# Attention and experts on one core: each half expert serves all four batches in one pass, with the input parts streamed from DRAM

## The chip, the core and the metric

The kernel runs on one core of a Trainium2 chip. The metric is the device time of one execution in microseconds (us). Three executions of the kernel before gave 2418.21, 2427.02 and 2414.76 us, median 2418.21 us. One more execution was taken with the profiler; its time was 2428.88 us and its span, from the first instruction to the last, 2427.1 us.

Five engines work side by side, each through its own list of instructions in order: PE (TensorE, the matmuls), DVE (VectorE), ACT (ScalarE), POOL (GpSimd) and SP (SyncE, which here issues all the transfers). PEld is the loading of a matmul's stationary operand.

## What is computed

```python
# attention: B, H, S, D = 4, 8, 768, 64 with 16 clusters
mask = q_assign[:, :, :, None] == k_assign[:, :, None, :]
attn = softmax(where(mask, q @ k.T / sqrt(D), -1e9))
x = (attn @ v) as [B * S, H * D] = [3072, 512]
# mixture of experts: E, DM, DF = 8, 512, 1024
P = exp(x @ w_gate - max)
for _ in range(8):
    P /= P.sum(1, keepdims=True) + 1e-9
    P /= P.sum(0, keepdims=True) + 1e-9
    P *= N / E
out = sum over e of P[:, e:e+1] * (relu(x @ w1[e]) @ w2[e])
```

The gates P are normalised eight times by rows (over the experts) and by columns (over all 3072 tokens of all four batches), so that no gate is known before the attention of the last batch has ended.

## The kernel before, in words

**Attention** comes first, head after head, and leaves each batch's output transposed in `xT`; `out_batch` (line 934) stores it to DRAM (`xd`), takes the logits of its gates, and for batch 0 alone its largest magnitude (`amx`, line 940), from which `first_x` makes the operands of batch 0 while attention still runs. In the same time `scan_first` (line 975) reads the weights of experts 0 and 1 once, for their largest magnitude.

**The experts** are split in two ways. Each matrix product is done by Strassen's scheme in the form with seven products: a 2 by 2 block product takes seven block matmuls ("pieces", m = 0 to 6 or n = 0 to 6) in place of eight, and pays with sums and differences of blocks. And each number is held as two float16 numbers, a high part (made on ACT) and a low part (what is left, made by a subtraction on DVE or POOL), so that a product takes three matmuls: high by high, high by low, low by high. So there are three preparations. Of a **weight** (`make_first`, line 1154, for w1; `make_second`, line 1197, for w2): load the raw block of 512 KB, scale it (ACT), four sums of blocks, and high and low parts of seven blocks in three steps (256, 512 and 1024 columns). Of the **input** of a batch (`next_x`, line 1282): four quarters `xq` are read from `xd`, four differences are taken, and seven parts `xs` (named B11, T1, T2, B22, T3, B21, T4) are split in high and low. Of the **hidden layer**: see below.

The work is a list of 64 **units** (line 1036): a unit is one batch b, one expert e and one half g of its 1024 hidden columns. A half expert is two weight tiles `wa` and two `wb` (f2 = 2g and 2g + 1). In each unit `layer1` (line 1334) runs seven pieces for each of two halves j, six matmuls of 384 columns each, 84 in all; `layer2` (line 1516) runs seven pieces in two parts, 18 matmuls of 256 columns a piece, 126 in all. Between them stand, for each j, on ACT the evictions `c` (line 1370) and the high parts of `h` (lines 1379 and 1388); on DVE the sums with the evicted products (`plus`, line 1373, three of them, one input in PSUM), three low parts of relu(c) (`split_raw`, line 1381, both inputs in SBUF) and four sums (`sums_of`, line 1464, both inputs in SBUF); on POOL or DVE four more low parts (`split_sum`, line 1390). `collect` (line 1546) adds each finished product, weighted by its gate, into the output on DVE (lines 1571 to 1577), 21 instructions a unit.

The 64 units are in two passes: batches 0 and 1 through all eight experts (32 units), then batches 2 and 3. Weights are made in the first pass, four tiles of each kind an expert, and stored to DRAM (`wd1`, `wd2`, 64 stores of 896 KB); the second pass loads them back (`load_first`, `load_second`, 64 loads). The input parts of two batches stay in SBUF for a whole pass. `scan` (line 1258) reads the raw weights of experts 2 to 7 again for their largest magnitude: eight loads of 512 KB and eight reductions on DVE (line 286) an expert.

**The gates** (line 1076): a maximum over all logits, an exponential, and eight rounds of seven DVE lines, two of which multiply the whole table `pr` (lines 1104 and 1119), with one small matmul (line 1111) for the column sums in the middle of each round.

**The order of the instructions** is set by a planner (lines 60 to 150) when the program is written. Each preparation is a process that asks for an engine with a cost in microseconds; the planner lets the engine that comes free first take the process with the smallest key (its due time), and the engines then keep that order. `LEAD` is the time, in the planner's clock, at which PE begins with the experts; `either(pool, dve)` offers a step to POOL and DVE, with a reluctance in microseconds added to DVE's. PE's own list is fixed: piece after piece of layer 1, and from piece 18 on one piece of layer 1 and one part of layer 2 by turns (`run_pe`, `LAG = 4`). The planner's costs are only what it plans with.

## Time and profile before

| | us |
|---|---|
| profiled execution | 2428.88 |
| its span | 2427.1 |
| median of three plain executions | 2418.21 |
| first matmul of the experts begins | 560.85 |
| last matmul of the experts begins | 2422.14 |
| PE busy in the span | 2295.4 (95%) |
| DVE busy | 2055.1 (85%) |
| POOL busy | 1278.9 (53%) |
| ACT busy | 1155.4 (48%) |

The profile's page gives busy times and the span in forty slices; other views of the same trace group instructions by line and shape in a stretch of time, list who waited for whom, follow the chain of waits that ended last, or give a table by stretches of time: busy time of each engine (with the number of its instructions in brackets), granted clock of PE as a share of full speed, busy share of the DMA engines, and GB/s. Times of instructions in a group may overlap by a few hundredths of a microsecond where one begins while the last one drains, so that a sum of them is somewhat more than the busy time.

### The profile page before, as it was taken

The numbers are of one execution on the slowest core, as the hardware profiler recorded it, in microseconds if no ns is written. First come the engines' busy times: TensorE is split into PE (matmuls) and PEld (weight loads), VectorE is DVE, ScalarE is ACT, GpSimd is POOL, SyncE is SP. The second block draws the span as 40 slices with busy tenths as digits, with TensorE's granted clock in tenths as the row PEclk, the third lists the DMA queues.
The fourth block names the chain that finished last, engine by engine and source line by source line (L and its number), as shares of the span: only waits on it lengthen the run. The fifth ranks groups of instructions, "written<-read, shape, count | busy, mean of one in ns | idle before, by whom it ended". The sixth has DMA issues, their size and how long they took to land.

```text
span 2427.1 us, 42887 instructions
## 1 busy us (share of the span) xinstructions
PE 2295.4 (95%) x16244; PEld 1618.8 (67%) x16244; DVE 2055.1 (85%) x3806; ACT 1155.4 (48%) x2300; POOL 1278.9 (53%) x1261
## 2 busy tenths in 40 slices
PE   6999999995899999999999999999999999999998
PEld 3655555552576677767776767777777777777776
DVE  7878777877999999999999999987777777777776
ACT  3554555554466555555555555443333333333332
POOL 4676766667678767666766666422232222222221
PEclk7999999997899999999999999999999999999999
DMA  8555454523234435343434223312111122112101
GB/s 186 132 128 142 94 121 90 136 71 137 98 116 152 145 121 171 119 153 122 144 122 139 96 94 124 118 61 92 62 62 62 62 79 90 61 67 72 62 31 53
DMA packets 145408, 254.02 MB, mean 105 GB/s; under 512 B 59592, under 2 KB 99632, under 8 KB 144688
## 3 DMA queue, kind: packets, MB, share of 16 engines
q1 hardware_dynamic: 145200, 251.28, 33.5%
q8 instruction: 127, 2.08, 0.4%
q14 instruction: 81, 0.66, 0.1%
HBM read 151.04 MB, written 71.30 MB: 92 GB/s over the span
## 4 chain that ended last, share of the span: by engine, by line
PE 69%; DVE 24%; issue 3%; ACT 1%; DMA 1%; SPq 1%; POOL 1%; DVEq 0%; ACTq 0%; POOLq 0%
PE a_ps L1350 15%; PE a_ps L1533 11%; PE ac_ps L1533 9%; PE c_ps L1533 8%; PE c_ps L1350 7%; DVE acc L1577 5%; PE av_ps L827 4%; PE b_ps L1350 4%; DVE c L1464 3%; PE max_ps L700 3%; DVE h L1381 3%; PE exp_ps L768 2%; PE exp_ps L769 2%; DVE mrt L704 2%; DVE c L1373 1%
## 5 line engine op out<-in xcount | busy, mean ns | idle before, releaser
L1533 PEld LDWEIGHTS <-h 128*128 128x128 f16 x8064 | 791.4, 98 | 225.9 <-issue 40.8
L1350 PEld LDWEIGHTS <-wa 128*128 128x128 f16 x5376 | 528.5, 98 | 288.3 <-issue 37.3
L1390 POOL TENSOR_TENSOR h<-s,h 128x384 f16<-128x384 f32 x128 | 130.3, 1018 | 712.0 <-ACT h L1388 697.8
L1379 ACT ACTIVATE h<-c 128x384 f16<-128x384 f32 x384 | 200.7, 523 | 536.0 <-DVE c L1373 535.6
L1350 PE MATMUL a_ps<-xsT,wa 128*128 128x384 f16 x2304 | 439.5, 327 | 13.8 <-ACT c L1370 7.0
L1533 PE MATMUL a_ps<-wb,h 128*128 128x256 f16 x3072 | 378.4, 273 | 12.8 <-DVE acc L1577 11.8
L1533 PE MATMUL ac_ps<-wb,h 128*128 128x256 f16 x2688 | 366.6, 273 | 3.2 <-DVE acc L1577 3.2
L1533 PE MATMUL c_ps<-wb,h 128*128 128x256 f16 x2304 | 288.1, 275 | 15.1 <-DVE acc L1577 12.3
L1577 DVE SCALAR_TENSOR_TENSOR acc<-a_ps,gates,acc 128x256 f32<-128x256 f32 x472 | 216.3, 476 | 81.9 <-PE a_ps L1533 80.8
L1381 DVE SCALAR_TENSOR_TENSOR h<-c,h 128x384 f16<-128x384 f32 x384 | 250.7, 655 | 8.6 <-ACT h L1379 8.6
L794 POOL TENSOR_TENSOR psum<-psum,pe 128x512 f32<-128x512 f32 (+1 forms) x208 | 221.2, 1082 | 53.1 <-ACT pe L775 38.4
L775 ACT ACTIVATE pe<-exp_ps 128x512 f32<-128x512 f32 x288 | 166.1, 597 | 126.3 <-PE exp_ps L769 109.0
L1390 POOL TENSOR_TENSOR h<-c,h 128x384 f16<-128x384 f32 x190 | 207.9, 1105 | 30.8 <-ACT h L1388 26.4
L1577 DVE SCALAR_TENSOR_TENSOR acc<-ac_ps,gates,acc 128x256 f32<-128x256 f32 x412 | 196.0, 476 | 30.9 <-PE ac_ps L1533 27.1
L704 DVE TENSOR_REDUCE mrt<-max_ps 128x1 f32<-128x512 f32 (+1 forms) x288 | 189.1, 682 | 27.3 <-PE max_ps L700 25.4
L1577 DVE SCALAR_TENSOR_TENSOR acc<-c_ps,gates,acc 128x256 f32<-128x256 f32 x352 | 155.4, 475 | 39.8 <-PE c_ps L1533 39.7
L1388 ACT CAST h<-c 128x384 f16<-128x384 f32 x256 | 130.1, 509 | 94.6 <-DVE c L1464 93.4
L1370 ACT ACTIVATE c<-a_ps 128x384 f32<-128x384 f32 x256 | 124.8, 487 | 88.3 <-PE a_ps L1350 86.5
L1350 PE MATMUL c_ps<-xsB,wa 128*128 128x384 f16 x768 | 148.5, 330 | 11.7 <-ACT c L1370 11.7
L1350 PE MATMUL b_ps<-xsB,wa 128*128 128x384 f16 x768 | 147.8, 329 | 0.0
L1350 PE MATMUL a_ps<-xsB,wa 128*128 128x384 f16 x768 | 146.7, 328 | 0.0
L1350 PE MATMUL c_ps<-xsT,wa 128*128 128x384 f16 x768 | 146.7, 328 | 0.0
(240 smaller groups left out, 3656.7 us busy)
## 6 DMA issues: line engine op xcount, KB each, us to landing
raw<-in_moe_w SPq DMA_DIRECT2D x112, 512.0 KB
wda<-wa SPq DMA_DIRECT2D x32, 896.0 KB
wdb<-wb SPq DMA_DIRECT2D x32, 896.0 KB
wa<-wda SPq DMA_DIRECT2D x32, 896.0 KB
wb<-wdb SPq DMA_DIRECT2D x32, 896.0 KB
scan<-in_moe_w SPq DMA_DIRECT2D x32, 256.0 KB
qn<-in_q SPq DMA_DIRECT2D x16, 384.0 KB
kn<-in_k SPq DMA_DIRECT2D x16, 384.0 KB
```

Source lines behind the costliest of these rows:

```text
L704: nc.vector.tensor_reduce(out=t["mr"][:, i0 : i0 + ni, ni - 1], in_=ps.rearrange("p (x c) -> p x c", x=ni), axis=AX, op=ALU.max)
L775: nc.scalar.activation(pe, ps.rearrange("p (x c) -> p x c", x=ni), AF.Exp, scale=SCALE)
L794: (nc.gpsimd if e == POOL else nc.vector).tensor_tensor(out=st[:, a:z], in0=old[a], in1=part, op=ALU.add)
L827: nc.tensor.matmul(av[o, a:z], vn[:, i, :], heads[t]["pe", c][:, i - i0], start=(i == 0), stop=False, skip_group_check=True)
L1350: nc.tensor.matmul(ps[:, 0:HB], wt[:, w_, a, c, :], xt[:, x_, c, :], start=(n in (0, 1, 5) and s_ == 0), stop=(s_ == len(steps) - 1), skip ...
L1370: nc.scalar.activation(t, ps[:, 0:HB], func, scale=KAPPA)
L1379: nc.scalar.activation(t[:, 0], c, AF.Relu)
L1381: nc.vector.scalar_tensor_tensor(out=t[:, 1], in0=c, scalar=0.0, in1=t[:, 0], op0=ALU.max, op1=ALU.subtract)
L1388: nc.scalar.copy(t[:, 0], c)
L1390: by(w).tensor_tensor(out=t[:, 1], in0=c, in1=t[:, 0], op=ALU.subtract)
L1533: nc.tensor.matmul(view(m, i), t[:, a_, i * P : (i + 1) * P], w[:, b_, x, :], start=(opens and n == 0 and i in (0, 2)), stop=(n == 5), ski ...
L1577: nc.vector.scalar_tensor_tensor(out=to, in0=src, scalar=gate[b, e][:, ti : ti + 1], in1=to, op0=ALU.mult, op1=ALU.add)
```

## The change

1. **One pass.** Units are ordered by expert: expert 0 batch after batch, both halves each; then for each expert and half the four batches, by turns downwards (3, 2, 1, 0) and upwards. A half expert's weights are made once, serve four units in a row and are dropped. The 64 stores and 64 loads of made weights are gone.
2. **Input parts streamed.** The seven parts of every batch are stored once in DRAM (`xsd`, 28 stores of 384 KB) and read back, seven loads of 384 KB, for each unit whose batch differs from the last one's (45 of the units: 315 loads). There are eleven places in SBUF for seven parts: each load takes the place of a part whose last use is over. Batches 1, 2 and 3 are split in the first units, one after the other, in the spaces of an output tile that isn't used yet; their split scales the quarters first (ACT) and takes low parts by a plain subtraction on POOL or DVE.
3. **Gates later and wider.** The gates begin 40 us later in the planner's clock, leave 2 us (`ROOM`) around each of their steps on PE, and do their two products of the whole table on POOL.
4. **The start.** `LEAD` is 32 in place of 25, and the planner takes the other engines as partly busy before it. The largest magnitude is taken of batches 0, 1 and 2 during attention (`LARGEST`), of batch 3 later. Expert 1 is scanned among the experts, no longer during attention.
5. **POOL or DVE.** From unit 8 on the reluctance towards DVE is 1.5 in place of 0.3. Raw blocks have three places in place of four, and the outputs of all four batches stay in SBUF.

The core of the diff:

```diff
-LEAD = 25.0
+LARGEST = 2
+LEAD, LOGITS, ROOM = 32.0, 40.0, 2.0
...
-            if b == 0:
+            if b <= LARGEST:
                 yield DVE, 3.3
+                amx = sm.tile([P, 1], F32, name="amx")
                 largest(amx, xts[b].rearrange("p c s -> p (c s)"))
...
-        for e in range(2):
-            plan.spawn(scan_first(e), urgency("values", nheads - 12 + 4 * e))
+        plan.spawn(scan_first(0), urgency("values", nheads - 12))
...
+    NRAW, NH = 3, 20
...
-    for c in range(B // 2):
-        for e in range(E):
-            turns = [(j, g) for g in range(NG2) for j in range(2)] if e else [(j, g) for j in range(2) for g in range(NG2)]
-            units += [(2 * c + j, e, g) for j, g in turns]
+    units = [(b, 0, g) for b in range(B) for g in range(NG2)]
+    for e in range(1, E):
+        for g in range(NG2):
+            turn = range(B - 1, -1, -1) if g % 2 == 0 else range(B)
+            units += [(b, e, g) for b in turn]
     NU = len(units)
+    FULL = NG2 * B
...
     def gates():
+        yield LOGITS
...
-            yield DVE, 0.4
-            nc.vector.tensor_tensor(out=pr, in0=pr, in1=r.unsqueeze(2).broadcast_to([P, NTT, E]), op=ALU.mult)
+            yield POOL, 0.6
+            nc.gpsimd.tensor_tensor(out=pr, in0=pr, in1=r.unsqueeze(2).broadcast_to([P, NTT, E]), op=ALU.mult)
...
             yield t_g
+            yield ROOM
             yield PE, 0.15
             ps = g_tile()
             nc.tensor.matmul(ps[:, 0:E], ones, c, start=True, stop=True)
+            yield ROOM
...
-    def either(pool, dve, reluctance=0.3):
-        return (POOL, pool), (DVE, dve, reluctance)
+    def either(pool, dve):
+        return (POOL, pool), (DVE, dve, 0.3 if ev["slot", FULL].time is None else 1.5)
...
-        yield SP, 0.6
-        nc.sync.dma_start(out=wd1[idx], in_=t.rearrange("p x a c f -> p (x a c f)"))
...
+    spots = [(3, r, q) for r in (1, 2) for q in (1, 2)]
+    t_spot = Tokens(len(spots))
...
     def next_x(b):
...
+        for o in XQ:
+            yield ev["xq", b, o]
+            yield ACT, 0.93
+            nc.scalar.activation(xq[o], xq[o], AF.Copy, scale=sx[:, b : b + 1])
+        for i, o in enumerate(XS):
             for t in LESS.get(o, ()):
                 w = yield either(2.25, 0.87)
                 less(*t, by(w))
+            yield t_spot
             yield ACT, 0.93
+            t = xs[b][o] = accp.tile([P, 2, KC, HB], F16, name=f"xt{b}{o}", tag=f"acc3{r}{q}")
+            nc.scalar.copy(t[:, 0], xq[o])
+            w = yield either(1.9, 0.9)
+            by(w).tensor_tensor(out=t[:, 1], in0=xq[o], in1=t[:, 0], op=ALU.subtract)
+            yield SP, 0.6
+            nc.sync.dma_start(out=xsd[b, o], in_=t.rearrange("p x c s -> p (x c s)"))
...
+    def load_x(u):
+        b = units[u][0]
+        if u > first_of[b] + 1:
+            yield from after(u - 2)
+        for n, o in enumerate(XS):
+            yield ev["xsd", b, o]
+            urgent(piece_time(u, n) - 9)
+            yield t_x
+            yield SP, 0.6
+            tag = free_x.pop(0)
+            t = xt[u, o] = pers.tile([P, 2, KC, HB], F16, name=f"x{u}{o}", tag=tag)
+            nc.sync.dma_start(out=t.rearrange("p x c s -> p (x c s)"), in_=xsd[b, o])
...
+        if j == 1 and u + 1 < NU and units[u + 1][0] != b:
+            free_x.append(xtag[u, x])
+            t_x.put(plan)
```

The planner makes the new order. At the start of the experts, DVE's list right behind the last sum of unit 0 (the row `c<-b_ps`), before (`pr`, `rsum` and `csum` are the gates' tables, `xs` and `xq` the parts of batch 1):

```order
L1373 SCALAR_TENSOR_TENSOR c_6476<-b_ps,c_6476 128x384
L1104 TENSOR_TENSOR pr<-pr,rsum 128x192
L307 SCALAR_TENSOR_TENSOR xsT_6537<-xqB_6270,sx,xsT_6537 128x768
L1107 TENSOR_REDUCE csum<-pr 128x8
L1464 SCALAR_TENSOR_TENSOR c_6371<-c_6371,s_6490 128x384
L1381 SCALAR_TENSOR_TENSOR h<-c_6504,h 128x384
L1381 SCALAR_TENSOR_TENSOR h<-c_6488,h 128x384
L1114 TENSOR_SCALAR csum_6594<-g_ps 128x8
L1115 RECIPROCAL csum_6594<-csum_6594 128x8
L1116 TENSOR_SCALAR csum_6594<-csum_6594 128x8
L1464 SCALAR_TENSOR_TENSOR s_6600<-c_6476,h_6560 128x384
```

The same place of DVE's list after the change (lines have moved: 1373 is 1429, 1381 is 1437, 1464 is 1520; 1262 is the low part of a `wb`, 1337 that of an input part):

```order
L1429 SCALAR_TENSOR_TENSOR c_6356<-b_ps,c_6356 128x384
L1437 SCALAR_TENSOR_TENSOR h<-c_6394,h 128x384
L1262 TENSOR_TENSOR wb<-raw,wb 128x256
L1124 TENSOR_SCALAR gneg<-g_ps 128x1
L1337 TENSOR_TENSOR xt1T_6396<-xqB_6191,xt1T_6396 128x768
L1520 SCALAR_TENSOR_TENSOR s_6466<-c_6356,h_6451 128x384
L1437 SCALAR_TENSOR_TENSOR h<-c_6371,h 128x384
L1520 SCALAR_TENSOR_TENSOR h_6451<-c_6371,h_6451 128x384
L1520 SCALAR_TENSOR_TENSOR c_6371<-c_6371,s_6466 128x384
L1520 SCALAR_TENSOR_TENSOR c_6394<-c_6394,c_6371 128x384
L1262 TENSOR_TENSOR wb<-sums,wb 128x1024
```

Before, the gates' third round stood between the hidden layer's steps here; now the gates are only at their maximum, and parts of weights stand there. From the logits to the last sum of unit 1 (the fourth row `c<-b_ps`) DVE had 146 instructions and has 82; from there to the last sum of unit 4 it had 150 and has 199.

The second place is POOL's list in the middle of the experts, before (`wa` and `sums` are weights, `h` the hidden layer's low parts):

```order
L1390 TENSOR_TENSOR h<-c_9748,h 128x384
L1181 TENSOR_TENSOR sums<-raw,sums 128x256
L1181 TENSOR_TENSOR sums<-raw 128x256
L1181 TENSOR_TENSOR sums<-sums,raw 128x256
L1189 TENSOR_TENSOR wa<-raw,wa 128x256
L1181 TENSOR_TENSOR sums<-raw 128x256
L1181 TENSOR_TENSOR sums<-raw,sums 128x256
L1189 TENSOR_TENSOR wa<-raw,wa 128x512
```

And after the change, in the middle of a later expert:

```order
L1446 TENSOR_TENSOR h<-h_19712,h 128x384
L1262 TENSOR_TENSOR wb<-sums,wb 128x1024
L1446 TENSOR_TENSOR h<-c_19597,h 128x384
L1446 TENSOR_TENSOR h<-c_19624,h 128x384
L1446 TENSOR_TENSOR h<-s_19895,h 128x384
L1446 TENSOR_TENSOR h<-h_19884,h 128x384
L1446 TENSOR_TENSOR h<-c_19776,h 128x384
L1446 TENSOR_TENSOR h<-c_19802,h 128x384
```

A unit has eight of these low parts of `h`. In the whole program POOL took 434 of the 512 before and takes 505 now; DVE took 78 and takes 7. The weights' sums and low parts were on DVE in 62 places and are in 16.

270 lines of the change are left out of this document (143 added, 127 removed).

## The prediction

> **What bounds the kernel now.** I read the slices of the page first, then the table by stretches, then who waited, then the groups of instructions by shape. In the page's forty slices (attention is the first nine or so) PE is full nearly everywhere, and DVE is full from slice 11 to slice 25 and less so afterwards:
>
> ```profile
> PE   6999999995899999999999999999999999999998
> DVE  7878777877999999999999999987777777777776
> ```
>
> The table by stretches says how much PE got done in each (start and end in us, length, then busy time and instructions of PE, PEld, DVE, ACT and POOL, PE's granted clock, busy share of the DMA engines, GB/s):
>
> ```profile
> 560.00:645.00 85.00, 50.50 (x266) 30.17 (x267) 77.28 (x147) 41.33 (x70) 66.12 (x55) 0.74 0.34 119
> 645.00:700.00 55.00, 55.00 (x425) 41.27 (x423) 48.87 (x96) 32.34 (x66) 32.47 (x34) 1.00 0.32 110
> 700.00:1500.00 800.00, 765.51 (x5758) 564.92 (x5756) 760.77 (x1340) 437.21 (x828) 552.59 (x493) 0.99 0.38 130
> 1500.00:1600.00 100.00, 97.32 (x738) 72.04 (x737) 95.42 (x177) 49.42 (x93) 46.36 (x37) 1.00 0.33 113
> 1600.00:2300.00 700.00, 700.00 (x5368) 524.98 (x5366) 545.68 (x1087) 267.41 (x561) 186.20 (x178) 1.00 0.20 71
> ```
>
> A unit has 84 + 126 = 210 matmuls. From 1600 to 2300 us, in the second pass, 5368 / 210 = 25.56 units took 700 us: 27.39 us a unit, with PE never idle. That is the floor, and the change leaves PE's work as it is. From 700 to 1500 us 5758 / 210 = 27.42 units took 800 us, 29.18 each; at the floor they'd have taken 751, so 49 us were lost there, and 3.7 more from 1500 to 1600 (738 matmuls are 96.3 us of work). From 645 to 700 nothing was lost (425 matmuls are 55.4 us). The stretch 560 to 645 holds the experts' start, with more of layer 1 than of layer 2, so I count by line (matmuls of that line, and by the chain what six of the one and six of the other take):
>
> ```profile
> 560.00:645.00 85.00, 37.10 (x162) 0.74 0.34 119
> 560.00:645.00 85.00, 12.76 (x82) 0.74 0.34 119
> ```
>
> ```profile
> 645.45 0.98 PE a_ps L1350 x6
> 646.43 0.66 PE ac_ps L1533 x6
> ```
>
> 162 x 0.163 + 82 x 0.110 = 35.4 us of work in 84 us (the first matmul is at 560.85): 49 us lost. All in all PE loses about 102 us among the experts, half at the start and half in the first pass. What it waits for at the start, by the timeline, and in the first pass, by the list of waits (total, times, longest):
>
> ```profile
> 607.39 2.08 PE L1350 MATMUL c_ps<-xsB,wa 128*128 128x384 f16 x6 [10.77 <-ACT c L1370]
> ...
> 635.21 0.60 PE L1111 MATMUL g_ps<-csum,ones 128*128 128x8 f32 x2 [7.28 <-DVE csum L1107]
> ```
>
> ```profile
> PEld L1533 <- issue: 36.7, 37, 2.9
> ```
>
> At the start PE stands before the gates' small matmuls and behind evictions that stand behind DVE; the six matmuls after such a wait take 2.08 us, about twice the usual, and the granted clock of the stretch is 0.74. In the first pass it stands before the loads of `h`, which DVE and POOL make. DVE is the engine behind both: 77.28 of 85 us, and 760.77 / 27.42 = 27.75 us a unit in the first pass against 545.68 / 25.56 = 21.35 in the second.
>
> **Part 1: the middle of the experts (units 5 to 60).** In the first pass a unit carries two sets of weights, later one. Three things change DVE's 21.35 us. The largest magnitudes of the weights come back, and low parts of `h` leave it:
>
> ```profile
> L286 DVE TENSOR_REDUCE am<-raw 128x1 f32<-128x1024 f32 x42 | 50.6, 1204 | 0.0
> L1464 DVE SCALAR_TENSOR_TENSOR c<-c,s 128x384 f32<-128x384 f32 x54 | 54.4, 1007 | 0.3
> L1464 DVE SCALAR_TENSOR_TENSOR s<-c,h 128x384 f32<-128x384 f32 x55 | 51.1, 929 | 0.6 <-ACT h L1370 0.6
> L1464 DVE SCALAR_TENSOR_TENSOR h<-c,h 128x384 f32<-128x384 f32 x55 | 42.3, 769 | 0.3
> L1381 DVE SCALAR_TENSOR_TENSOR h<-c,h 128x384 f16<-128x384 f32 x164 | 121.4, 745 | 2.5 <-ACT h L1379 2.4
> ```
>
> The same groups in the second pass (1700 to 2300 us, 22 units):
>
> ```profile
> L1381 DVE SCALAR_TENSOR_TENSOR h<-c,h 128x384 f16<-128x384 f32 x131 | 72.0, 550 | 4.3 <-ACT h L1379 4.3
> L1464 DVE SCALAR_TENSOR_TENSOR c<-c,s 128x384 f32<-128x384 f32 x44 | 32.7, 743 | 0.6
> L1464 DVE SCALAR_TENSOR_TENSOR h<-c,h 128x384 f32<-128x384 f32 x44 | 24.3, 553 | 1.3
> L1464 DVE SCALAR_TENSOR_TENSOR s<-c,h 128x384 f32<-128x384 f32 x44 | 24.1, 548 | 0.0
> L1390 DVE TENSOR_TENSOR h<-c,h 128x384 f16<-128x384 f32 x22 | 21.9, 994 | 1.1 <-ACT h L1388 1.1
> ```
>
> The scans are 56 over 56 units: +1.2 us. One low part of `h` a unit moves to POOL: -1.0. The third is a lengthening: these instructions read two tiles of SBUF, and they last longer where POOL is busier: six times 0.195, twice 0.264, 0.381 and 0.216, together 2.9 us a unit, between POOL's 186 / 700 = 27% and its 553 / 800 = 69%. POOL's load after the change, from its own rows:
>
> ```profile
> L1390 POOL TENSOR_TENSOR h<-c,h 128x384 f16<-128x384 f32 x73 | 78.9, 1090 | 14.3 <-ACT h L1388 14.2
> L1232 POOL TENSOR_TENSOR wb<-sums,wb 128x1024 f16<-128x1024 f32 x28 | 65.3, 2333 | 3.8 <-ACT wb L1230 3.4
> L1224 POOL TENSOR_TENSOR sums<-raw 128x256 f32<-128x256 f32 x47 | 40.6, 866 | 94.3 <-PE a_ps L1533 58.9 <-ACT raw L1213 35.5
> L1232 POOL TENSOR_TENSOR wb<-raw,wb 128x512 f16<-128x512 f32 x26 | 34.4, 1323 | 3.0 <-ACT wb L1230 3.0
> ```
>
> Eight low parts of `h` at 1.09 and one set of weights (four sums and a low part of 256 columns at 0.87, one at 1.32, one at 2.33) make 8.7 + 8.0 = 16.7 us of 27.4, 61%. In proportion the lengthening is 2.9 x (61 - 27) / (69 - 27) = 2.3 us. DVE then has 21.35 + 1.2 - 1.0 + 2.3 = 23.9 us a unit, 87%; the fullest units have three scans, 26.3, still below 27.4. What does PE lose at that? Nothing at 21.35, 1.8 us a unit at 27.75. A straight line gives 0.7 us, 40 us over 56 units; a threshold gives none. I take 13: DVE no longer falls behind for good, but the heavy units follow one another. So the 53 us lost from 700 to 1600 become 13 (0 to 40), though they are now spread over all units, the once undisturbed second half too.
>
> The Trainium skill, "SBUF — State Buffer", "Who interferes with whom", speaks against this part: a DVE instruction with two SBUF inputs and a GpSimd instruction that reads SBUF exclude one another, for a whole instruction at a time. The trace agrees on who suffers (the rows above); how much follows below as a rival.
>
> The transfers lie beside all this. The 64 stores and 64 loads of 896 KB (115 MB) go, 28 stores and 315 loads of 384 KB (132 MB) come. A unit with a new batch needs 7 x 0.393 = 2.75 MB, with weights some 3.8 MB in 27.4 us, 139 GB/s, close to the 130 GB/s of the stretch 700 to 1500, where the DMA engines were 38% busy. The chip went faster:
>
> ```profile
> 640.00:650.00 10.00, 9.50 (x69) 6.77 (x68) 8.29 (x25) 3.77 (x8) 2.70 (x3) 0.92 0.88 301
> ```
>
> At 301 GB/s a part takes 1.3 us, at 130 it takes 3. With eleven places for seven parts, a place is read for the last time eleven pieces before it is needed again, 11 x 1.96 = 21 us. So I cost the parts at nothing; uncovered, 45 changes of batch at 3 us would be 135 us. On SP's queue each such load waits for a piece of PE, as the loads of made weights did, and raw weights stand behind it; such a wait is over as soon as PE is where the plan has it. The stores that go are worth nothing: what PE waits for (above) is DVE, ACT and `h`, not transfers.
>
> **Part 2: the start (units 0 to 4).** From the logits to the last sum of unit 1, DVE's list falls from 146 instructions to 82. Groups of the stretch 560 to 645:
>
> ```profile
> L1119 DVE TENSOR_TENSOR pr<-pr,csum 128x192 f32<-128x192 f32 x7 | 7.6, 1080 | 0.0
> L307 DVE SCALAR_TENSOR_TENSOR xsT<-xqB,sx,xsT 128x768 f16<-128x768 f32 x4 | 5.7, 1417 | 0.0
> L1104 DVE TENSOR_TENSOR pr<-pr,rsum 128x192 f32<-128x192 f32 x8 | 5.2, 650 | 0.0
> L1101 DVE TENSOR_SCALAR rsum<-rsum 128x24 f32<-128x24 f32 x8 | 4.9, 611 | 0.0
> L307 DVE SCALAR_TENSOR_TENSOR xsB<-xqB,sx,xsB 128x768 f16<-128x768 f32 x3 | 4.2, 1385 | 0.0
> L1107 DVE TENSOR_REDUCE csum<-pr 128x8 f32<-128x192 f32 x8 | 3.9, 489 | 0.0
> L286 DVE TENSOR_REDUCE am<-xqB 128x1 f32<-128x768 f32 x4 | 3.7, 941 | 0.0
> L1189 DVE TENSOR_TENSOR wa<-raw,wa 128x512 f16<-128x512 f32 x1 | 2.2, 2199 | 0.2 <-ACT wa L1187 0.2
> ```
>
> Out go the gates' products (12.8 us, to POOL), six of eight rounds of lines 1101 and 1107 (three quarters of 8.8, 6.6; five shorter lines I leave out, against the overlap of such times), and batch 1's split and magnitude (13.6): 33 us. In come five plain splits (at 1.4, 7.0), a difference (1.4), three weight parts of 1024 columns, two of 512 and two of 256 more, three low parts of `h` (0.75 each) and a scan (1.2). The 512 is 2.2 a piece. The 1024 was never on DVE: between one and two of the 512, 2.2 to 4.4; POOL's 2.33 is the nearest row and I take it. That is 7.0 + 1.4 + 7.0 + 4.4 + 0.9 + 2.2 + 1.2 = 24 us. So DVE saves 9 of its 77 us, and PE's loss by the end of unit 1 falls from 49 to 40; with the other ends of these prices, by some 8 us more or less.
>
> In units 2 to 4 the gates return: six rounds, each with 1.1 us of lines 1101 and 1107 and about as much for the short ones, 13 us, and three more scans (3.6). From 645 to 700 us DVE had 55 - 48.9 = 6.1 us free, which makes 9 in the 82 us of three units. So it has up to 8 us too much; since units 5 to 8 are lighter and PE runs some pieces ahead, I take 3. A round now crosses from DVE to POOL and back twice: DVE's next sum of columns waits behind POOL's product, which stands behind low parts of weights, and behind DVE's sum stand evictions of PE's pieces. Two us of spacing before PE covers one such part (2.33). Loss at the start: 43 us (25 to 49).
>
> **Part 3: attention.** Two more reductions of a whole batch, sixteen scans of expert 1 fewer:
>
> ```profile
> L286 DVE TENSOR_REDUCE amx<-xT x1: 3333/3333/3333, 207.0 to 207.0; 128x1 f32<-128x3072 f32 x1
> ```
>
> ```profile
> L286 DVE TENSOR_REDUCE am<-scan x32: 662/672/686, 28.6 to 241.9; 128x1 f32<-128x512 f32 x32
> ```
>
> +6.7 and -10.8 us of DVE, which is not full there. Cost 0 (-4 to +4).
>
> **The sum.** Lost before 49 + 53 = 102, after 43 + 13 = 56: 46 us less. The profiled execution took 2428.88 us (span 2427.1), 0.4% above the median of 2418.21; 2428.88 - 46 = 2382.9, and scaled to the median (x 0.9956) 2372 us.
>
> **The rivals.** A measurement of this kernel tells about 0.5% (12 us) from no change.
>
> *DVE stays full* (chance 0.14): the line holds, 40 us lost in the middle, and the start gains nothing, 49. Gain 13 us: 2405. For it: heavy units in a row. Against: 26.3 us even then.
>
> *POOL becomes the bound, slower* (0.11). The two sets of a half expert's `wa` or `wb` fall into two of four units: there POOL has 8.7 + 16 = 24.7 us of 27.4, and all low parts of `h` stand in that one queue behind parts of 2.33 us. If `h` then reaches layer 2 more than four steps late (4 x 1.96 = 7.8 us), half of 56 units lose twice the first pass's 1.8 us: 100 us in the middle, 143 in all against 102, 2459. For it: PE's longest waits in the first pass were before loads of `h`, at 69% POOL. Against: on average POOL has less to do than then.
>
> *Full exclusion* (0.07). If each of 14 such DVE instructions waits out what is left of a POOL instruction, that is the sum of squares over twice the time: (8 x 1.09² + 5 x 0.87² + 1.32² + 2.33²) / 54.8 = 0.37 us, 5.2 a unit. Some 1 us of it is in the second pass's 21.35 already, so DVE comes to 21.35 + 1.2 - 1.0 + 4.2 = 25.8, units with three scans to 28.2, above 27.4. By the line that loses 70 us, with 43 at the start 113: 2429, no change that can be told. Against: with 6.2 low parts of `h` and some 1.7 sets a unit on POOL the first pass gives 6.2 us by this sum, and the rows give 2.9 above the second pass's 1.
>
> That is the rule of "Who interferes with whom" (the Trainium skill) taken at its word; the trace so far bears out some 60% of it.
>
> *Input parts late, slower* (0.04): each of 45 changes of batch 2 us late is 90 us, 2462; it is slower than before from 1.3 us a change. The 21 us speak against it.
>
> *Better than forecast* (0.08): nothing lost in the middle, 25 at the start: 2342.
>
> **How the numbers follow.** The forecast has the other 0.56. The range 2338 to 2406 takes in the forecast with its bounds, the better case and the first rival, 0.78. Faster by over 0.5% (below 2406): 0.56 + 0.08 + 0.11 of the first rival = 0.75. Within: 0.03 of it and the third, 0.10. Slower: 0.15.
>
> **What would show it.** After the change, windows past unit 8 with 760 or more matmuls per 100 us in both halves, DVE near 87% and POOL near 61%; the three lines 1429, 1437, 1520 as long as here or up to 0.25 us longer; the start's loss mostly on DVE still, without waits of PE before the gates' matmuls. Wrong: fewer than 740 per 100 us anywhere past unit 8; PE's waits on transfers; POOL full with PE before loads of `h`.

## The result, and the profile after

The changed kernel takes 2357.8 us (median of 4 runs, 2355.9 to 2360.1), the kernel before 2417.9 in the same comparison: a ratio of 0.9746, 95% interval 0.9718 to 0.9774. It is faster by 60 us, where 46 were forecast (2372 us, range 2338 to 2406). The profiled execution took 2356.5 us, 72.4 less than the one profiled before.

The page's slices of the changed kernel, PE and DVE, as shown before the change:

```profile
PE   6999999996899999999999999999999999999998
DVE  7887788877998898879788977888798879877776
```

DVE is no longer full for fourteen slices on end, and its load is now nearly the same to the end. The table by stretches of the changed kernel (columns as in the prediction):

```profile
560.00:645.00 85.00, 66.36 (x454) 45.46 (x453) 81.82 (x139) 48.85 (x90) 71.48 (x62) 0.96 0.41 135
645.00:700.00 55.00, 50.96 (x378) 37.30 (x376) 49.49 (x120) 22.95 (x45) 23.90 (x25) 0.97 0.38 127
700.00:1500.00 800.00, 796.33 (x6096) 596.05 (x6095) 674.47 (x1267) 394.83 (x786) 478.04 (x444) 1.00 0.36 113
1500.00:1600.00 100.00, 100.00 (x769) 74.96 (x767) 88.00 (x166) 47.43 (x94) 55.68 (x52) 1.00 0.39 126
1600.00:2300.00 700.00, 700.00 (x5363) 524.46 (x5362) 571.41 (x1093) 328.11 (x656) 396.03 (x371) 1.00 0.35 109
```

6096 matmuls are 29.03 units of 27.39 us, 795 us of work in the 800 from 700 to 1500; from 1500 on nothing is lost. The start has again to be counted by line. These are the windows 540 to 645, 645 to 700 and 700 to 800 us of the changed kernel, line 1406 (layer 1) and then line 1589 (layer 2):

```profile
540.00:645.00 105.00, 52.49 (x258) 26.42 (x258) 0.92 0.44 150
645.00:700.00 55.00, 28.30 (x144) 14.42 (x144) 0.97 0.38 127
700.00:800.00 100.00, 55.78 (x294) 28.66 (x294) 1.00 0.27 93
```

```profile
540.00:645.00 105.00, 29.00 (x221) 22.40 (x222) 0.92 0.44 150
645.00:700.00 55.00, 28.53 (x222) 21.70 (x220) 0.97 0.38 127
700.00:800.00 100.00, 55.93 (x441) 42.96 (x440) 1.00 0.27 93
```

With 0.163 and 0.109 us a matmul (84 and 126 of them make a unit of 27.4), 258 and 221 matmuls are 66.1 us of work. The experts begin earlier than before, and then stand still, as PE's timeline shows (the first pieces, and two longer waits):

```profile
543.66 0.81 PE L1406 MATMUL a_ps<-xsB,wa 128*128 128x384 f16 x4
...
555.10 2.08 PE L1406 MATMUL a_ps<-xsT,wa 128*128 128x384 f16 x6 [6.46 <-ACT c L1426]
...
577.94 2.08 PE L1406 MATMUL a_ps<-xsT,wa 128*128 128x384 f16 x6 [3.61 <-ACT c L1426]
```

From 543.66 to 645 us that is 35.2 us lost, then 7.3 to 700 and 4.0 to 800 (46.5 together, with matmuls on a border counted on both sides; counted once, 47.1). The same count is made below for every kernel that was run. It divides the 72.4 us between the two profiled executions: the experts begin 17.2 us earlier (560.85 to 543.66), PE loses 47.1 us instead of 54.5 up to 800 us (7.4), and 1.4 instead of 47.5 from 800 to 2300 us (46.1). The remaining 1.7 lie behind 2300 us.

### The profile page after: what moved, and what is told of

Its sections match the earlier page's. It is cut to its first block, busy times and chain, and to the rows that moved or that the text cites. A ratio compares the mean times of both kernels' runs of the same rounds, so it can differ in the third digit from the quotient of the medians.

```text
span 2354.7 us, 43336 instructions
## 1 busy us (share of the span) xinstructions
PE 2266.0 (96%) x16244; PEld 1612.8 (68%) x16244; DVE 1952.4 (83%) x3652; ACT 1153.5 (49%) x2303; POOL 1416.9 (60%) x1408
## 3 DMA queue, kind: packets, MB, share of 16 engines
q8 instruction: 127, 2.08, 0.4%
## 4 chain that ended last, share of the span: by engine, by line
PE 86%; DVE 9%; POOL 2%; DMA 2%; issue 1%; ACT 1%; SPq 0%; DVEq 0%; ACTq 0%; POOLq 0%
PE a_ps L1406 20%; PE a_ps L1589 14%; PE ac_ps L1589 12%; PE c_ps L1589 10%; PE c_ps L1406 10%; PE b_ps L1406 5%; PE av_ps L850 4%; PE max_ps L723 2%; PE exp_ps L791 2%; DVE mrt L727 2%; PE exp_ps L792 2%; PE misc_ps L583 1%; DMA kn<-in_k 1%; DVE vsum L533 1%; DVE am L308 1%
## 5 line engine op out<-in xcount | busy, mean ns | idle before, releaser
L1437 DVE SCALAR_TENSOR_TENSOR h<-c,h 128x384 f16<-128x384 f32 x384 | 267.3, 697 | 9.0 <-ACT h L1435 8.9
L1446 POOL TENSOR_TENSOR h<-c,h 128x384 f16<-128x384 f32 x254 | 252.8, 1008 | 24.7 <-ACT h L1444 22.3
L817 POOL TENSOR_TENSOR psum<-psum,pe 128x512 f32<-128x512 f32 (+1 forms) x213 | 228.0, 1086 | 54.7 <-ACT pe L798 47.8
L727 DVE TENSOR_REDUCE mrt<-max_ps 128x1 f32<-128x512 f32 (+1 forms) x288 | 189.9, 682 | 27.9 <-PE max_ps L723 26.1
L1446 POOL TENSOR_TENSOR h<-h,h 128x384 f16<-128x384 f32 x123 | 140.5, 1142 | 38.2 <-PE c_ps L1589 23.8
L850 PE MATMUL av_ps<-pe,vn 128*64 128x512 f32 (+1 forms) x768 | 135.1, 494 | 0.4 <-ACT xT L870 0.4
L723 PE MATMUL max_ps<-kX,qX 96*128 96x256 f32 (+1 forms) x384 | 124.4, 389 | 7.5 <-DVE mrt L727 6.3
L792 PE MATMUL exp_ps<-qX,kX 98*128 98x512 f32 (+1 forms) x384 | 127.2, 344 | 0.0
L1426 ACT ACTIVATE h<-a_ps 128x384 f32<-128x384 f32 x128 | 62.5, 488 | 103.4 <-PE a_ps L1406 103.3
```

What stands on the lines that cost most here:

```text
L723: nc.tensor.matmul(ps[:, y * (z - a) : (y + 1) * (z - a)], t["qa"][0:96, i * P : (i + 1) * P], t["k2"][0:96, a:z], start=True, stop=True)
L727: nc.vector.tensor_reduce(out=t["mr"][:, i0 : i0 + ni, ni - 1], in_=ps.rearrange("p (x c) -> p x c", x=ni), axis=AX, op=ALU.max)
L792: nc.tensor.matmul(o, t["k2"][0:98, ki], t["qa"][0:98, a:z], start=False, stop=True)
L817: (nc.gpsimd if e == POOL else nc.vector).tensor_tensor(out=st[:, a:z], in0=old[a], in1=part, op=ALU.add)
L850: nc.tensor.matmul(av[o, a:z], vn[:, i, :], heads[t]["pe", c][:, i - i0], start=(i == 0), stop=False, skip_group_check=True)
L1426: nc.scalar.activation(t, ps[:, 0:HB], func, scale=KAPPA)
```

## The experiments

**Theory.** PE loses time where DVE has too much to do for each unit of PE's 27.4 us; the change spreads the making of the weights over all units, so DVE falls below the load at which PE waits. At the start, what leaves DVE and PE's own queue counts. **Rivals.** The gain is that 115 MB of transfers go (made weights stored and loaded); or it is only the shift of work to POOL (the planner's reluctance of 1.5); or attention became shorter.

All counts in one table: where the experts' first matmul begins, the matmuls of layer 1 and 2 up to 800 us and PE's loss from that begin to 800, the loss from 800 to 2300 us (1500 less matmuls / 210 x 27.39), and the ratio to the kernel before.

| kernel | begin, us | matmuls to 800 | lost to 800, us | lost 800-2300, us | ratio (95%) |
|---|---|---|---|---|---|
| before | 560.85 | 619, 768 | 54.5 | 47.5 | 1 |
| before_again | 557.19 | 630, 784 | 54.7 | 46.5 | one execution |
| changed | 543.66 | 696, 879 | 47.1 | 1.4 | 0.9746 (0.9718-0.9774) |
| stores_back | 545.35 | 672, 844 | 53.1 | 1.6 | 0.9762 (0.9743-0.9780) |
| reluct_low | 547.55 | 678, 855 | 48.7 | 4.2 | 0.9772 (0.9758-0.9785) |
| before_reluct | 552.44 | 654, 815 | 52.1 | 16.0 | 0.9869 (0.9845-0.9893) |
| dose2 | 547.29 | 686, 864 | 46.7 | 23.8 | 0.9848 (0.9827-0.9869) |
| dose2_spread | 548.77 | 679, 858 | 47.0 | 25.6 | 0.9872 (0.9855-0.9888) |
| dose4 | 549.47 | 678, 855 | 46.8 | 57.6 | 0.9991 (0.9978-1.0005) |
| gates_old | 543.27 | 642, 796 | 65.3 | 1.1 | 0.9828 (0.9810-0.9845) |
| scans_old | 550.56 | 645, 804 | 56.7 | 1.4 | 0.9815 (0.9801-0.9829) |
| scan1_first | 546.60 | 702, 882 | 42.8 | 1.2 | 0.9737 (0.9713-0.9761) |
| split_later | 538.87 | 678, 856 | 57.3 (see below) | 1.4 | 0.9767 (0.9753-0.9780) |
| gates_later | 544.44 | 678, 851 | 52.3 | 1.1 | 0.9766 (0.9742-0.9790) |

### The middle

**stores_back.** In `make_first` and `make_second` of the changed kernel:

```diff
+        yield SP, 0.6
+        nc.sync.dma_start(out=wd1[e * NP2 + f2], in_=t.rearrange("p x a c f -> p (x a c f)"))
+        plan.copied(4.5)
```

> The changed kernel, with the 64 stores of made weights (896 KB each, 57 MB) put back; nothing reads them. Theory (the middle's gain is DVE's load per unit, which falls below PE's 27.4 us): no change from the changed kernel, 0.975 of the time before, within 0.003; over 760 matmuls per 100 us past unit 8 still. Rival (the gain is that transfers go): half of the transfers that went come back, so about half of the 50 us that the middle gained, 0.983 to 0.988.

Measured: 0.9762. Past 800 us it loses 1.6 us, as little as without the stores: the stores that went are no part of the middle's gain. The loads that went were not put back. In the kernel before they were issued from 1450 us on, and from 1600 to 2300 us, with loads all along, that kernel lost nothing.

Up to 800 us stores_back loses 53.1 us, 6 more than the changed kernel, with one wait of 11.1 us before a matmul of the gates. With the stores the planner wrote another order of the start (DVE's list differs from 560 us on), so these 6 us can't be laid to the stores alone. In dose2 and reluct_low, below, the order up to 800 us is that of the changed kernel, and they lose 46.7 and 48.7 us there: so far apart are executions of one order.

**reluct_low** (the changed kernel) and **before_reluct** (the kernel before) each change one number:

```diff
-        return (POOL, pool), (DVE, dve, 0.3 if ev["slot", FULL].time is None else 1.5)
+        return (POOL, pool), (DVE, dve, 0.3)
...
-    def either(pool, dve, reluctance=0.3):
+    def either(pool, dve, reluctance=1.5):
```

> The changed kernel, with the planner's reluctance to give work to DVE kept at 0.3 throughout (the change raises it to 1.5 from unit 8 on). By the order of instructions 62 go from POOL to DVE, about one a unit. Theory (threshold of DVE at 27.4 us): DVE has some 0.9 us a unit more, 23.3 to 24.1, so no change from the changed kernel, 0.975 of the time before within 0.004. Rival (the middle's gain is the shift to POOL): a good part of the middle's 50 us comes back, 0.983 or more.

> The kernel before, with one number changed: the planner's reluctance to give work to DVE rather than POOL is 1.5 in place of 0.3, from the first unit on. By the order of instructions, 134 of DVE's go, 117 of them to POOL. Theory (DVE's load alone): DVE's first pass falls from 27.75 by 134 x 0.9 / 32 = 3.8 to some 24 us a unit, and most of the 53 us lost from 700 to 1600 us goes: 0.978 to 0.985 of the time before. Rival (the weights' work must be spread over all units, since POOL takes the place of DVE): POOL comes to 20.2 + 3.7 = 23.9 of 27.4 us a unit in the first pass, PE waits for h from POOL, and it is 0.993 to 1.01.

Measured: without the shift the changed kernel keeps nearly all of its gain (0.9772, 4.2 us lost past 800). With the shift alone the kernel before gains 31.5 of 47.5 us past 800, and 0.9869 in time. So either way serves, and they don't add up: both take load from DVE, and once it is low enough more brings nothing. The rival for before_reluct (POOL takes DVE's place) fell, although it did not reach the theory's 0.985 either.

**dose2, dose4.** In the changed kernel, after `s1` (dose2), and after `s1` and `s4` (dose4) of each half unit:

```diff
+    def more(k):
+        if k[0] >= 8:
+            nc.vector.tensor_reduce(out=extra, in_=ident.unsqueeze(1).broadcast_to([P, 8, P]), axis=AX, op=ALU.max)
...
         ev["s1", k].set(plan)
+        more(k)
```

> The changed kernel, with two more reductions on DVE (128 x 1024, some 1.2 us each, of a constant tile, their result unused) in every unit from unit 8 on, in places where nothing else is moved. DVE then has 22.4 to 23.2 + 2.4 = 24.8 to 25.6 us a unit. Theory (a threshold at PE's 27.4 us): 0 to 10 us more than the changed kernel, 0.975 to 0.979 of the time before. Rival (the prediction's straight line, 0.28 us of PE for each us of DVE): 2.4 x 0.28 x 56 = 38 us more, 0.990.

> The same with four reductions a unit: DVE has 27.2 to 28.0 us a unit, at or above PE's 27.4. Theory (threshold): 56 units lose what DVE has above 27.4, up to 0.6 each, and heavy units with two or three scans can no longer be made up for: 20 to 60 us more than the changed kernel, 0.983 to 0.999 of the time before, DVE at 97% or more past unit 8. Rival (straight line): 4.8 x 0.28 x 56 = 75 us more, 1.006.

Measured: 23.8 and 57.6 us lost past 800, ratios 0.9848 and 0.9991. Neither expectation held for dose2: it lost more than a threshold at 27.4 us allows and less than the straight line. The loss of dose4 lies in the theory's bounds, but with DVE busy for 93% (800 to 1500 us), not the 97% that this theory needs. DVE was full around the scans in dose2 (10.0 us of 10 from 1300 to 1310 us, with PE at 8.6), so I mended the theory (only full stretches lose) and held the scans apart.

**dose2_spread.** On top of dose2:

```diff
-            urgent(slot_time(s - 7) + 8.0 * (i + 1))
+            if e > 1:
+                yield from after(s - 10 + i)
+                urgent(slot_time(s - 10 + i) + 14)
```

> The kernel of dose2 (the changed kernel with two more reductions a unit on DVE), with the eight scans of each expert from the third on held apart, one a unit (each waits for the unit it belongs to, from ten units ahead), where dose2 has all eight within some 100 us. DVE's work is the same but for a few parts that the planner gives to POOL. Theory, mended after dose2 (PE loses only in stretches in which DVE is full, there the units with two or three scans): DVE's 25 to 25.6 us a unit then hold everywhere, and most of dose2's 24 us past 800 us go: 0.976 to 0.980 of the time before. Rival (loss follows DVE's mean load, wherever the scans stand): dose2's 0.985 within 0.002.

Measured: 25.6 us lost past 800, as in dose2: holding the scans apart brought nothing, and the forecast of the mended theory fell. That the loss follows DVE's mean load and nothing else is not shown by this. In stretches of 20 us from 800 to 2300 us, 18.1 of the 19.5 us in which PE stood idle in dose2 lie in or right behind a stretch with DVE at 95% or more (a third of all stretches); in dose2_spread it is 10.9 of 17.9, again in a third. So the scans are not all that fills DVE. And the added reductions stand right behind `s1`, ahead of the hidden layer's other sums, so that they also lengthen the chain that ends in `h`. PE's longest rows of waits from 800 to 2300 us, in dose2, dose4 and dose2_spread:

```profile
PE c_ps L1596 <- DVE acc L1636: 16.7, 11, 1.6
```

```profile
PE c_ps L1597 <- DVE acc L1637: 27.8, 18, 2.5
```

```profile
PE c_ps L1416 <- ACT c L1436: 9.9, 8, 1.5
```

In dose2 and dose4 PE waits until DVE has added a product to the output (`collect`). In dose2_spread it waits for an eviction on ACT; the one at 1224.61 us stands behind a high part of `h` that waited for a sum on DVE, with an added reduction just ahead of that sum. How much of the doses' loss is load and how much is this chain stays open.

DVE's mean load of each kernel can be read from the stretch 800 to 1500 us (columns as above; in turn before, before_reluct, changed, reluct_low, dose2, dose2_spread, dose4):

```profile
800.00:1500.00 700.00, 669.70 (x5034) 494.12 (x5032) 667.45 (x1173) 375.93 (x709) 473.78 (x421) 0.99 0.37 126
```

```profile
800.00:1500.00 700.00, 691.28 (x5265) 514.45 (x5263) 651.03 (x1141) 388.77 (x738) 551.04 (x518) 1.00 0.39 134
```

```profile
800.00:1500.00 700.00, 700.00 (x5363) 524.43 (x5361) 589.72 (x1111) 337.79 (x668) 416.23 (x392) 1.00 0.37 116
```

```profile
800.00:1500.00 700.00, 697.77 (x5340) 522.26 (x5339) 610.01 (x1135) 337.51 (x663) 385.95 (x357) 1.00 0.37 115
```

```profile
800.00:1500.00 700.00, 689.58 (x5269) 515.15 (x5267) 621.68 (x1140) 330.49 (x655) 399.17 (x383) 1.00 0.36 114
```

```profile
800.00:1500.00 700.00, 690.28 (x5263) 514.55 (x5261) 627.70 (x1139) 331.14 (x654) 395.02 (x383) 1.00 0.36 112
```

```profile
800.00:1500.00 700.00, 680.80 (x5146) 505.02 (x5144) 648.79 (x1160) 324.82 (x642) 394.21 (x378) 0.99 0.34 108
```

Divided by their units (matmuls / 210):

| kernel | DVE, us a unit | PE, us a unit | lost, us a unit |
|---|---|---|---|
| changed | 23.1 | 27.4 | 0.0 |
| reluct_low | 24.0 | 27.5 | 0.1 |
| dose2 | 24.8 | 27.9 | 0.5 |
| dose2_spread | 25.0 | 27.9 | 0.5 |
| before_reluct | 26.0 | 27.9 | 0.5 |
| dose4 | 26.5 | 28.6 | 1.2 |
| before | 27.8 | 29.2 | 1.8 |

The loss begins near 23.5 us, 86% of PE's unit, and then grows by some 0.4 us for each us of DVE ((1.81 - 0.51) / (27.84 - 24.78) = 0.42). From 1600 to 2300 us dose2 lies on this line too (24.1 us, 0.3 lost). But the line is rough: before_reluct lies 0.5 us below it, and dose4 from 1600 to 2300 us (26.1 us, 0.8 lost) 0.3 us. That before_reluct has no added reduction in the chain to `h` would fit; no run separates it.

### The start

**gates_old.** The function `gates` of the kernel before in the changed kernel (no spacing, all products on DVE, begun at once).

> The changed kernel, with the gates as before: begun at once, no room kept before their small matmuls, their 16 products on DVE. Theory (the start's gain is what leaves DVE and PE there): 12.8 us of products are DVE's again and PE stands before the gates' matmuls: 8 to 18 us more than the changed kernel, 0.978 to 0.982 of the time before, with waits of PE before matmuls of csum in the first 90 us of the experts. Rival (the start's gain has nothing to do with the gates, DVE is full there either way): within 0.002 of the changed kernel's 0.975.

Measured: 0.9828, just above the theory's 0.982, and 65.3 us lost up to 800 instead of 47.1. PE's list of waits, 545 to 645 us, of gates_old (total, times, longest):

```profile
PE g_ps L1138 <- DVE csum L1134: 18.9, 5, 12.6
PE g_ps L1116 <- DVE g L1113: 9.9, 1, 9.9
```

PE stands 28.8 us in front of the gates' small matmuls; in the changed kernel there is no such wait. The part on the gates is worth some 18 us; its three pieces (later, spaced, products on POOL) were put back together and are not told apart.

**scans_old** puts the magnitudes back, **scan1_first** only those of expert 1's weights:

```diff
-LARGEST = 2
+LARGEST = 0
...
-        plan.spawn(scan_first(0), urgency("values", nheads - 12))
+        for e in range(2):
+            plan.spawn(scan_first(e), urgency("values", nheads - 12 + 4 * e))
...
-        if e > 0:
+        if e > 1:
             plan.spawn(scan(e), lead + slot_time(uses[e, 0][0] - 8))
```

(scan1_first keeps `LARGEST = 2`; in both `scale` of expert 1 is set before the experts begin.)

> The changed kernel, with the magnitudes as before: in attention those of batch 0 and of experts 0 and 1, and those of batch 1 among the first pieces of the experts. It tells where the experts' earlier begin comes from (at 543.7 us in the profile of the changed kernel, 560.9 before). Theory (the attention part is worth 0 to 4 us; most of the 17 us is that the execution profiled before ran its attention at lower granted clocks): the experts begin at 540 to 548 us, and the time is 0.973 to 0.977 of the time before. Rival (the sixteen scans made attention longer): they begin at 553 or later, and the time is 0.980 or more.

> The changed kernel, with the magnitudes of expert 1's weights back in attention (sixteen scans there, as before), those of batches 1 and 2 left there as the change has them. It divides what scans_old gave back. Theory (what cost was the magnitudes of batches 1 and 2 among the experts, a chain ahead of their splits): no such cost here; DVE has eight reductions of 1.2 us fewer in the first units, so 0 to 9 us less than the changed kernel, and the longer attention takes 0 to 6: 0.971 to 0.976 of the time before, PE's loss from 530 to 800 us 37 to 46 us. Rival (the cost was the sixteen scans in attention): the experts begin at 550 us or later, and 0.977 to 0.981.

Measured: 0.9815 and 0.9737. The time of scans_old is the rival's, but its begin, 550.6 us, is neither way's. scan1_first came out as its theory has it. scans_old and scan1_first differ from one another only in the magnitudes of batches 1 and 2: 13.9 us of the loss up to 800 (56.7 against 42.8) and 4.0 us of the begin. So what cost in scans_old was not the sixteen scans but these magnitudes among the experts, in two places. PE's timeline of scans_old, the end of attention and the first pieces with batches 2 and 3:

```profile
541.83 0.26 PE L921 MATMUL misc_ps<-ident_r,rr 128*24 128x128 f32 x1 [4.02 <-DVE am L1318]
...
688.42 1.15 PE L1407 MATMUL c_ps<-x4B,wa 128*128 128x384 f16 x6 [2.69 <-DMA x4B<-xsd2B] 
702.72 1.32 PE L1407 MATMUL a_ps<-x4T,wa 128*128 128x384 f16 x6 [3.70 <-DMA x4T<-xsd2T] 
```

The same step of attention in the changed kernel:

```profile
537.57 0.22 PE L921 MATMUL misc_ps<-ident_r,rr 128*24 128x128 f32 x1 [1.03 <-DVE rr L917]
```

In scans_old the experts' reductions stand on DVE between the small steps that end attention, so that the way from attention's last sum over the values to the experts' first matmul takes 15.3 us; in scan1_first and the changed kernel it takes 10.6 and 9.7. And the splits of batches 2 and 3, which wait for their magnitudes, come so late that PE waits for parts from DRAM: "input parts late", a rival of the prediction that did not come to pass in the change itself (but for one wait of 1.0 us for a part of batch 3), because it finds those magnitudes in attention.

**split_later**, a test of the wait of 6.46 us at 548.6 us, where an eviction on ACT stands behind a split:

```diff
-        plan.spawn(next_x(b), lead + slot_time(first_of[b]) - 60)
+        plan.spawn(next_x(b), lead + slot_time(first_of[b]) - (30 if b == 1 else 60))
```

> The changed kernel, with one number changed: the splits of batch 1's input parts are due 30 us before their first unit, not 60, so that they don't stand in ACT's and POOL's queues before the first evictions. Theory (the 6.46 us that PE stood at 548.6 us was an eviction on ACT behind a split that waited for a difference on POOL): this wait goes, and as DVE is full at the start a part of it comes back later: 0 to 6 us less than the changed kernel, 0.972 to 0.975 of the time before. Rival (DVE's list alone sets the start): no change, 0.975 within 0.001; or later splits hold up unit 2: 0.976 to 0.980.

Measured: 0.9767, with an interval that overlaps the changed kernel's; no gain. The time is that of the last of the expected ways, but the trace shows another reason. The wait did shrink, from 6.46 to 0.86 us, as PE's timeline of split_later shows:

```profile
555.34 1.14 PE L1406 MATMUL a_ps<-xsT,wa 128*128 128x384 f16 x6 [0.86 <-ACT c L1426]
```

The 57.3 us in the table can't be held against 47.1: here the experts' first pieces run inside the end of attention, whose last matmuls come at 552 us, so attention's own steps count as loss. Unit 5 begins at 705.5 us, in the changed kernel at 706.2. What puts split_later behind comes after that, on ACT and then on PE:

```profile
710.92 9.69 ACT L1640 ACTIVATE acc<-acc,gates 128x256 f32<-128x256 f32 x24 [0.29 <-DVE gates L1166]
```

```profile
721.76 2.08 PE L1406 MATMUL a_ps<-x4T,wa 128*128 128x384 f16 x6 [7.04 <-ACT c L1426]
```

All 24 scalings of the first two batches' sums by their gates stand in one row ahead of an eviction. In the changed kernel 19 of them stand so, for 7.9 us, and PE's wait there is 2.62 us. That later splits cost anything is not shown.

**gates_later**, an attempt at a faster version:

```diff
-            urgent(14.0 + 11 * it)
+            urgent(14.0 + 18 * it)
...
-        plain = b < 2 and e == 0
+        plain = b < 3 and e == 0
...
-            if b < 2 and e == 1 and g == 0 and m == SOON[d]:
+            if b < 3 and e == 1 and g == 0 and m == SOON[d]:
```

> The changed kernel, with the gates' eight rounds due 18 us apart instead of 11, and batch 2, like batches 0 and 1, summed without its gates in expert 0 and scaled afterwards on ACT, so that no sum waits for them before unit 6. Theory (DVE's list is what PE loses the start to): the same work in a longer stretch where DVE is less full, 0 to 12 us less than the changed kernel, 0.970 to 0.975 of the time before; PE's loss from 645 to 800 us (11 us in the changed kernel) falls below 6. Rival (the start's loss is made by the first two units alone): no change, 0.975 within 0.002.

Measured: 0.9766, 18.5 us lost from 645 to 800 instead of 11.3. A new wait took the place of the old ones. ACT's timeline and PE's in gates_later:

```profile
736.59 9.68 ACT L1640 ACTIVATE acc<-acc,gates 128x256 f32<-128x256 f32 x24 [1.78 <-DVE gates L1166]
```

```profile
747.42 2.08 PE L1406 MATMUL c_ps<-x6B,wa 128*128 128x384 f16 x6 [8.67 <-ACT c L1426]
```

The late gates release 24 scalings at once on ACT, and an eviction that PE waits for stands behind all of them.

**before_again.**

> The kernel before once more, for a second profile of its attention. Theory (the execution profiled first had a slow attention): the experts begin at 550 to 555 us, not at 560.9, and their loss is 98 to 106 us as in the first. Rival (the attention before is that long): 559 us or later.

Measured: the experts begin at 557.2 us, between what the theory and the rival gave, and lose 54.7 + 46.5 = 101.2 us. No version tried is faster than the changed kernel by more than the measurement tells; scan1_first's interval covers its ratio. The new `LEAD` and the places for raw blocks were not tried alone.

## Why the prediction was right, point by point

**The floor** held: 5363 matmuls in 700 us are 27.41 us a unit, with nothing lost past 800 us.

**Part 1, the middle**, was right in its mechanism: DVE has too much to do for each unit. One reading on the way was wrong. The row `PEld L1533 <- issue` names no releaser, and I took it for a wait for `h`. PE's own list of waits for the same stretch of the kernel before (660 to 1600 us) names DVE:

```profile
PE a_ps L1533 <- DVE acc L1577: 11.2, 15, 2.7
PE c_ps L1533 <- DVE acc L1577: 10.8, 8, 2.3
PE ac_ps L1533 <- DVE acc L1577: 2.6, 4, 0.8
```

PE stands until DVE has added a product to the output. Together with a smaller row that is 25.5 of the 36.5 us in that list. So PE waits for DVE directly, and this takes away the ground that the rival on POOL had, that PE's longest waits were for `h`.

Two sizes were off. DVE's load was set at 23.9 us a unit and came out at 23.1 (800 to 1500) and 571.41 / 25.54 = 22.4 (1600 to 2300). The scans make 0.4 us of the difference from 1600 us on (16 in 25.5 units, not one a unit), and the rest is the lengthening, which was set at 2.3 us. The groups of the changed kernel, 1600 to 2300 us, with POOL at 396 / 700 = 57%:

```profile
L1437 DVE SCALAR_TENSOR_TENSOR h<-c,h 128x384 f16<-128x384 f32 x153 | 99.5, 651 | 4.3 <-ACT h L1435 4.3
...
L1520 DVE SCALAR_TENSOR_TENSOR h<-c,h 128x384 f32<-128x384 f32 x51 | 44.3, 868 | 0.4
L1520 DVE SCALAR_TENSOR_TENSOR c<-c,c 128x384 f32<-128x384 f32 x51 | 41.1, 805 | 0.8
L1520 DVE SCALAR_TENSOR_TENSOR c<-c,s 128x384 f32<-128x384 f32 x51 | 39.5, 775 | 1.0
L1520 DVE SCALAR_TENSOR_TENSOR s<-c,h 128x384 f32<-128x384 f32 x51 | 32.2, 631 | 0.9 <-ACT h L1426 0.9
```

Against the second pass before it is six times 0.101, twice 0.315, 0.032 and 0.083, and twice -0.148 for the row that the prediction had left out; that one in the kernel before, 1700 to 2300 us:

```profile
L1464 DVE SCALAR_TENSOR_TENSOR c<-c,c 128x384 f32<-128x384 f32 x44 | 41.9, 953 | 0.8
```

Together 1.2 us, half of what proportion to POOL's share gave. The other size is how DVE's load becomes PE's loss. I stood between a line that begins at 21.35 and a threshold at 27.4; measured, it begins near 23.5 and rises by 0.4 per us. At 23.9 that gives 0.2 us a unit, about the 13 us that I took; at 22.4 to 23.1 it gives nothing. So the step "53 us become 13" came out as 5, of which 4.0 lie in units 5 and 6, before 800 us. POOL has 15.5 to 16.3 us a unit where 16.7 were worked out.

**The transfers** cost next to nothing, as forecast: in the changed kernel PE has no wait past 800 us and one of 1.0 us for an input part before, and stores_back shows that the stores that went gave nothing back in the middle.

**Part 2, the start**, has the right sum by luck. 43 us lost by the end of unit 4 were forecast, 40 of them by the end of unit 1. These are the stretches from the first matmul of unit 0 to that of unit 2 (168 matmuls of layer 1 and 90 of layer 2, which runs behind: 37.2 us of work), and from there to that of unit 5 (252 and 378, 82.3 us), before and after:

```profile
560.85:646.90 86.05, 52.24 (x280) 31.45 (x279) 78.36 (x151) 42.29 (x72) 66.12 (x55) 0.75 0.36 127
646.90:729.70 82.80, 82.80 (x636) 61.99 (x635) 74.38 (x148) 51.38 (x104) 54.51 (x55) 1.00 0.31 106
```

```profile
543.66:609.30 65.64, 45.52 (x267) 27.80 (x266) 61.55 (x89) 40.47 (x72) 54.62 (x47) 0.90 0.51 168
609.30:706.20 96.90, 87.23 (x650) 63.94 (x649) 89.63 (x197) 43.88 (x88) 58.32 (x54) 0.98 0.33 111
```

By the end of unit 1 PE had lost 48.9 us before and loses 28.4 now, not 40. In units 2 to 4 it had lost 0.5 and loses 14.6, not 3. The two errors are of the same size and cancel. DVE's work in units 2 to 4 was forecast well (74.4 + 16.6 = 91.0 us, 89.6 measured); the step at fault there is the price that I set for it, 3 us. In units 0 and 1 DVE saves 16.8 us where 9 were worked out, and PE no longer stands before the gates' small matmuls: gates_old has still lost 48.2 us when its unit 2 begins. In units 2 to 4 PE's list of waits names DVE's sums into the output for 8.5 us.

Undone by itself, the gates' part costs 18 us, since PE stands before the small matmuls while DVE works off its list, and the magnitudes of batches 1 and 2 cost 14 (scans_old against scan1_first). If the two add up, which no run tried, the new order without both would lose some 79 us up to 800, more than the old one.

**Part 3, attention**, failed in its step "cost 0 (-4 to +4)". The scans and reductions cost nothing that can be told: scans_old, with all of them as before, ends its last sum over the values at 535.2 us, the changed kernel at 534.0. What I left out is the chain behind that, from there to the experts' first matmul, in which experts' work already stands in the queues. In the kernel before it takes 14.6 us, in the changed kernel 9.7: a gain of 4.9. PE's timeline before and after (attention's last sum and the first piece of the experts):

```profile
546.29 0.62 PE L835 MATMUL av_ps<-nht,ve 4*128 4x512 f32 x2
...
560.85 1.48 PE L1350 MATMUL a_ps<-xsB,wa 128*128 128x384 f16 x4
```

```profile
533.97 0.61 PE L858 MATMUL av_ps<-nht,ve 4*128 4x512 f32 x2
...
543.66 0.81 PE L1406 MATMUL a_ps<-xsB,wa 128*128 128x384 f16 x4
```

The other 12.3 us of the earlier begin lie within attention. With the same attention the three executions of the kernel before and of before_reluct have that last sum at 546.3, 543.1 and 536.6 us, those with the changed attention between 532.4 and 539.1. A lower granted clock alone, as the expectation of scans_old has it, does not explain the late ends: from 0 to 500 us the clock was 0.94, 0.98 and 0.96 in those three and 0.95 in the changed kernel. How much of this is the change and how much the execution stays open; since 46.1 + 7.4 + 4.9 = 58.4 of the 60 us between the medians are accounted for, little is left for it.

**The sum.** 102 us lost should have become 56 and became 48.5: 7.5 us better. With the 4.9 us behind attention that is 12.4 of the 14 us by which the forecast was too slow.

**The rivals.** DVE is not full past 800 us (84% and 82%), and POOL does not bound (57 to 60%). Full exclusion: an instruction of line 1437 in the kernel before (1700 to 2300 us), and the same in the changed kernel (1600 to 2300 us; shortest, median, longest in ns):

```profile
L1381 DVE SCALAR_TENSOR_TENSOR h<-c,h x131: 544/548/559, 1700.3 to 2291.5; 128x384 f16<-128x384 f32 x131
```

```profile
L1437 DVE SCALAR_TENSOR_TENSOR h<-c,h x153: 537/549/2086, 1600.1 to 2298.4; 128x384 f16<-128x384 f32 x153
```

By their times in the trace, 109 of the 153 begin while POOL is idle and take 549 ns on average; 44 begin inside an instruction of POOL and take 901 on average, the longest 1.5 us more than the shortest. That is how the rule of the Trainium skill ("SBUF — State Buffer", "Who interferes with whom") has it, a whole instruction at a time, and the trace agrees with it there. But the 4.2 us a unit that I made of it rest on meetings at random, and 1.2 were measured: POOL is busy for 57% of the time, and only 29% of these instructions begin inside one of its own.

## What to carry to other kernels

Count, for each unit of the engine that bounds, what the next busiest engine has to do: here PE lost nothing with DVE at 84% of it, 0.1 us a unit at 88% and 0.5 at 90 to 95%, whether the scans came bunched or one a unit. Below that point further relief brought nothing, and before spending a rewrite on it, try the number that shifts work elsewhere: in the old kernel one number gave half of the gain (0.9869 against 0.9746). Ask more than one view which wait it is: a row that names no releaser was taken for `h` here, and another view of the same trace named DVE's sums. At a seam between stages look at the chain of small steps for what the next stage has already queued in front of them, and count it as time on the path.
